# k and q loaded as twelve rows of one head per partition, and transposed by quarters of the array

## The chip, the cores and the metric

One core of one Trainium2 chip runs the whole program. The metric is the device time of one execution in microseconds (us), lower is better. The kernel before took 157.97 us, the median of three runs (157.73, 158.18 and 157.97). A change of about 0.3% (0.5 us) is what a measurement can tell from none.

## The reference, cut to what matters

Two stages. The first is a causal attention over 4 batches and 8 heads (768 rows of 64 values each), in which each query row sees only six of the 24 key chunks of 32 rows. A chunk is chosen by an upper bound of its scores, from the smallest and the largest key values in it. The second is a soft mixture of experts over the 3072 rows of 512 that come out of the attention.

```python
ub = sum(max(q * k_min, q * k_max), -1)           # 768 x 24 per head
top_chunks = argsort(where(causal, ub, -1e9))[..., -6:]
attn = softmax(where(sel & causal, q @ k.T / 8, -1e9))
x = (attn @ v) as 3072 x 512
logits = x @ phi                                   # 3072 x 32 slots
slot_out = relu((softmax0(logits).T @ x) @ w1) @ w2     # 8 experts, 4 slots each
out = softmax1(logits) @ slot_out
```

The inputs are float32: q, k and v have 6.3 MB each, the weights 33.5 MB.

## The kernel before, in words

The attention works on 16 pairs of heads, in a pipeline. The order of all work is written out by hand: ORDER and PLAIN are lists of step names for each turn i of the pipeline, and every engine runs its instructions in that order. One turn works on several pairs at once: scores S0 to S5, exponentials E0 to E5 and diagonal masks A0 to A5 for pair i, the bounds and the choice of chunks (UB, SL, SH, UN, NT, NC) for pair i+1, the transposes of k and q with what follows them (KT, KE, KN, KX, BD and QT, QE, QP) for pair i+2, the loads of k and q (LK, LQ) for pair i+4 and of v (LV) for pair i+2, and the product with v (P0 to P5), its normalising (NO) and its transposes (XT, XE) for the pairs before.

**Loads.** `load` (L158) is one DMA, issued by GpSimd (POOL), for k or q of one pair. It converts float32 to bfloat16 on the way. Partition p gets rows 6p to 6p+5 of the first head and then the same rows of the second head: two pieces of 1536 bytes in HBM, of 768 bytes in SBUF, for each of 128 partitions. `load_first` (L166) brings pair 0 as float32 through SyncE (SP), and `cast_first` (L172) converts it on VectorE and ScalarE, half a tile at a time. Of k_in and q_in there are three buffers each. v comes in pieces of 256 bytes (L180), the expert weights in rows of 8 KB in HBM (L156); the last two weight tiles come in halves of columns, as eight smaller DMAs (L154), at a time when tiles of the attention have been given up. All of these go through POOL.

**Transposes.** `transposes` (L234) turns such a tile so that the 64 values of a row lie on partitions: head 0 on partitions 0 to 63, head 1 on 64 to 127. For each of six row indices g and each head h it issues one weight load (128 rows, 64 columns of the tile) and one matmul with the identity as moving operand (128 columns), into half h of the PSUM tile tr_ps. That makes 12 matmuls per tile, 24 per pair. `evac_T` (L246) is one ScalarE (ACT) instruction, which copies tr_ps to kT or qT and puts the rows back into order on the way: it walks over p outside and over the six g inside.

**What uses kT and qT.** The scores (L342) and the masks added to them (L352) run on 64 rows of the array for each head, into one of two PSUM tiles sc_ps; ACT takes the exponential of them (L365); POOL cuts the diagonal (L370). VectorE (DVE) takes chunk minima and maxima of kT (L259, L264) and splits qT by sign (L279, L282); the bounds follow on the tensor engine (L291, L297), then the choice of the chunks on DVE (L303, L307, L316).

**The end.** After the last pair come the slot inputs, the first expert layer (L770), the second (L810) in two column halves, and the output rows (L840, evacuated on L847 and L849, sent by SP on L853).

Of the kernel before, what the change touches and what calls it, by code (L numbers as in the profile page):

```python
# [11 lines left out]
BF16 = mybir.dt.bfloat16  # L12
# [8 lines left out]
NQT = 6  # L21
P = 128
S = 768
D = 64
# [15 lines left out]
for _g, _pieces in enumerate(GROUPS):  # L40
# [4 lines left out]

PLAIN = """S0 KT S1 E0 A0 E1 LQ NO UB S2 S3 P0 KE LK SL P1 P2 P3 P4 E2 E3 A2 A1 W XT SH QT UN S4 S5 QE LV KN E4
E5 A5 A3 XE KX NT P5 NC BD QP A4 LG LC"""
# [4 lines left out]
LV A4 QP A5 BD""",  # L52
    1: """LV KT S0 LQ S1 LK UB E0 S2 E1 NO S3 P0 P1 A0 P2 SL KE SH E2 QT P3 A1 XT UN XE S4 W S5 KN E3 QE E4 E5
A5 P4 A2 KX A3 NT LG BD A4 NC P5 LC QP""",
    13: """S0 KT LV E0 S1 UB E1 A1 KE NO S2 S3 E2 E3 P0 P1 SL UN QT SH P2 QE P3 A3 A2 KN KX XT S4 S5 CL XE QP
E4 A0 W BD E5 P4 NT A5 LG P5 NC A4 LC MX""",
    14: """S0 E0 S1 UB S2 NO MT S3 RM P0 E1 E2 P1 E3 MB SL A1 A2 MS S4 MD A0 SH E4 UN P2 RS S5 XT P3 P4 A3 NT
NC E5 XE RE CU A4 A5 P5""",
    15: """NO S0 S1 C0 E0 S2 E1 P0 S3 E2 E3 V0 A1 XT P1 P2 A3 S4 A0 S5 P3 E4 A4 A2 E5 ME A5 P4 P5 XE""",
    16: """ZN0 ZPA ZP3 ZCT ZP4 D0 ZLH ZX0 ZN1 ZP5 Ze0 ZN2 D1 ZX1 ZL1 ZX2 D2 Ze1 ZL3 ZE2 ZL4 ZPM Zk ZPT ZMB D3  # L60
# [7 lines left out]
def kernel(  # L68
# [10 lines left out]
    nc = tc.nc  # L79
# [8 lines left out]
    EARLY = 12  # L88
    OLD = B - 1
    NO = OLD * NQT  # L90
    LAST = NPAIR - 1

    ctx.enter_context(tc.manual_schedule())
# [6 lines left out]
    p_tp = ps_ctx.enter_context(tc.tile_pool(name="p_tp", bufs=2, space=PSUM))  # L100
    st = {}
# [3 lines left out]
    ident = static.tile([P, P], BF16, name="ident")  # L105

    phi_sb = static.tile([P, NDG, NS], BF16, name="phi_sb")
    cT_all = static.tile([P, B * NQT, P], BF16, name="cT_all")
    c_pad = static.tile([P, NO, 4, CH], BF16, name="c_pad")
    lg_all = static.tile([P, OLD, NQT, NS], F32, name="lg_all")  # L110
# [28 lines left out]
    inp = l_ctx.enter_context(tc.tile_pool(name="inp", bufs=3, side="right"))  # L139
# [18 lines left out]
    def load(i, nm):  # L158

        b, j = divmod(i, NPB)  # L160
        t = inp.tile([P, 2, NQT * D], BF16, name=nm + "_in", tag=nm + "_in")
        src = {"k": k, "q": q}[nm][b, 2 * j:2 * j + 2]
        nc.gpsimd.dma_start(out=t, in_=src.rearrange("h (p g) d -> p h (g d)", p=P))  # L163
        st[nm, i] = t

    def load_first(nm):  # L166
        n = NQT * P // 2
        t = cT_all.rearrange("p t c -> p (t c)").bitcast(F32)[:, (nm == "q") * 2 * n:][:, :2 * n]
        st[nm + "f"] = t = t.rearrange("p (h x) -> p h x", h=2)
        nc.sync.dma_start(out=t, in_={"k": k, "q": q}[nm][0, :2].rearrange("h (p g) d -> p h (g d)", p=P))  # L170

    def cast_first(nm):  # L172
        t = inp.tile([P, 2, NQT * D], BF16, name=nm + "_in", tag=nm + "_in")
        nc.vector.tensor_copy(t[:, 0], st[nm + "f"][:, 0])  # L174
        (nc.scalar.copy if nm == "k" else nc.vector.tensor_copy)(t[:, 1], st[nm + "f"][:, 1])
        st[nm, 0] = t

    def load_v(i):
# [5 lines left out]


    load_first("k")
    load_first("q")
    for t in (ns_t[1], ns_t[0], caus, qgrp, headsel, squad):
        nc.vector.memset(t, 0.0)
# [8 lines left out]
    for n in "I K1 Q1 K2 Q2 W G M".split():  # L198
        if n[0] == "I":
            make_identity(nc, ident)  # L200
        elif n[0] == "W":
            load_w(0)
        elif n[0] == "V":
            load_v(int(n[1]))
        elif n == "G":
            nc.gpsimd.affine_select(
                out=qgrp, in_=qgrp, compare_op=ALU.not_equal, fill=1.0, base=0,
                pattern=[[-1, 4], [0, CH]], channel_multiplier=1,
            )
            nc.gpsimd.affine_select(  # L210
                out=caus[:4], in_=caus[:4], compare_op=ALU.is_ge, fill=NEG, base=0,
                pattern=[[0, 4], [-1, 4]], channel_multiplier=1,
            )
        elif n == "M":
            nc.gpsimd.affine_select(
                out=squad, in_=squad, compare_op=ALU.not_equal, fill=-NEG, base=0,
                pattern=[[-CH, 2], [-64, 2], [-1, NCHUNK]], channel_multiplier=1,
            )
            nc.gpsimd.affine_select(
                out=squad, in_=squad, compare_op=ALU.not_equal, fill=1.0, base=-NCHUNK,  # L220
                pattern=[[-CH, 2], [-64, 2], [0, NCHUNK]], channel_multiplier=1,
            )
        else:
            load(int(n[1]), n[0].lower())
# [8 lines left out]

    def transposes(i, nm):  # L234

        ps = p_tp.tile([P, NQT, P], BF16, name="tr_ps", tag="tp")
        src = st.pop((nm, i))
        for g in range(NQT):
            for h in range(2):
                nc.tensor.matmul(  # L240
                    ps[h * 64:(h + 1) * 64, g, :], lhsT=src[:, h, g * D:(g + 1) * D], rhs=ident,
                    is_transpose=True,
                )
        st[nm + "ps", i] = ps

    def evac_T(i, nm):  # L246

        t = tp3.tile([P, S], BF16, name=nm + "T", tag=nm + "T")
        nc.scalar.activation(  # L249
            t.rearrange("d (p g) -> d p g", g=NQT),  # L250
            st.pop((nm + "ps", i)).rearrange("d g p -> d p g"),
            func=ACT.Copy, scale=-1.0 if nm == "q" else 1.0,
        )
        st[nm + "T", i] = t
# [130 lines left out]
    def pv(i, ts):  # L385
        if i == LAST and ts[0] == 0:
            st["at", i] = p_tp.tile([P, 2, 3 * (D + 1)], F32, name="at_ps", tag="tp")
        elif i == LAST and ts[0] == 3:
            st["at_a"] = st["at", i]
            st["at", i] = last_home()[:, 0, :].rearrange("p (h c) -> p h c", h=2)  # L390
        elif ts[0] == 0:
            st["at", i] = p_at.tile([P, 2, 512], F32, name="at_ps", tag="at")
        at, tb = st["at", i], 3 if i == LAST and ts[0] > 2 else 0
        for t in ts:
            for h in range(2):
                o = at[:, h, (t - tb) * (D + 1):(t - tb + 1) * (D + 1)]
                for kg in range(t + 1):
                    g, c = BLOCK[(kg, t)]
                    nc.tensor.matmul(  # L399
                        o, lhsT=st["e", i, g][:, h, c:c + P], rhs=v_t[i % NV][:, h, kg, :],  # L400
                        start=(kg == 0), stop=(kg == t),
                    )
# [172 lines left out]
    def of(d, f, *a):  # L575
# [3 lines left out]
        "UB": of(1, ubound), "SL": of(1, search), "SH": of(1, shift), "UN": of(1, unselect),  # L579
        "NT": of(1, ns_transposes), "NC": of(1, evac_ns),  # L580
        "KT": of(2, transposes, "k"), "KE": of(2, evac_T, "k"), "KN": of(2, kmin), "KX": of(2, kmax), "BD": of(2, heads),
        "QT": of(2, transposes, "q"), "QE": of(2, evac_T, "q"), "QP": of(2, qsplit),
        "LK": of(4, load, "k"), "LQ": of(4, load, "q"), "LV": of(2, load_v), "Lv": of(1, load_v), "W": weights,
        "NO": of(-2, normalise), "XT": of(-2, x_transposes), "XE": of(-2, evac_x),
        "LG": lambda i: moe(moe_logits, i - 2), "LC": lambda i: moe(moe_copy, i - 2),
        "PHI": phi_load, "kc": lambda i: cast_first("k"), "qc": lambda i: cast_first("q"), "MASK": spread_mask, "CL": close_loads, "CU": close_bounds,
    }
    for g in range(len(GROUPS)):
# [130 lines left out]
    def slots_z():  # L719
# [9 lines left out]
    STEP.update({n: (lambda i, f=f, a=a: f(*a)) for n, f, *a in (  # L729
        ("ZCT", close_T), ("ZCE", close_e), ("ZCI", close_i), ("ZN0", normalise, LAST - 1),  # L730
        ("ZPA", pv, LAST, [0, 1, 2]), ("ZP3", pv, LAST, [3]), ("ZP4", pv, LAST, [4]), ("ZP5", pv, LAST, [5]),
        ("ZX0", x_transposes, LAST - 1), ("ZE0", evac_x, LAST - 1, 0, NQT, nc.vector.tensor_copy),
        ("Ze0", evac_x, LAST - 1, 0, NQT, nc.scalar.copy),
# [173 lines left out]
```

## Time and profile before

One profiled execution; its own time was 157.73 us, with a span of 155.8 us between its first and its last instruction.

| what | value |
|---|---|
| time of the profiled execution | 157.73 us |
| its span | 155.8 us |
| granted TensorE clock, mean | 0.964 |
| bytes read from HBM | 52.49 MB |
| bytes written to HBM | 6.29 MB |
| matmuls of L240 (the transposes) | 384, 229 ns each |
| ACT copies of L249 | 32, 815 ns (q) and 805 ns (k) each |
| loads of k and q by POOL | 30, 192 KB each in SBUF |

How to read it: PE is the tensor engine's matmuls, PEld its weight loads. A line such as L240 is a line of the kernel before. In a list in order of time the first number is the start in us from the span's beginning, the second the duration; x12 stands for twelve instructions told in one row, from the first one's start to the last one's end. Matmuls are pipelined, so that the duration of one (219 ns) is far longer than the step from one to the next. GB/s of the DMA engines counts the bytes as they arrive: a load that converts reads twice as many.

### The profile page before, as it was taken

What the parts mean: (1) busy time and instruction counts of PE and PEld (TensorE: products, weight loads), DVE (VectorE), ACT (ScalarE), POOL (GpSimd) and SP (SyncE); (2) the same over time, 40 slices, a digit from 0 to 9 for tenths busy, and PEclk for the clock granted to TensorE, in tenths of its full rate; (3) what the DMA queues carried; (4) which work ended last, traced back from release to release, by engine and by line L of the source; (5) the groups of instructions that cost most, each with busy time, mean ns of one, the idle gap of its engine ahead of it and who ended that gap; (6) DMA issues with size and microseconds to landing.
All of it is one profiled execution on the core that took longest, in us unless ns stands there. A gap on an engine that the chain in (4) does not pass through costs nothing.

```text
span 155.8 us, 6234 instructions
## 1 busy us (share of the span) xinstructions
PE 135.7 (87%) x2591; PEld 95.5 (61%) x2591; DVE 117.0 (75%) x408; ACT 123.5 (79%) x165; POOL 98.3 (63%) x196
## 2 busy tenths in 40 slices
PE   6649899998999999999999999998999999877700
PEld 3335467766776777676767766685759856545400
DVE  5766979988889889898888989899946343439900
ACT  3669999999899999999989999998796303447900
POOL 7959895977789687796977885855627970000000
PEclk9956999999999999999999999999999999999995
DMA  4999999999999999999999999999999999998995
GB/s 161 176 207 199 168 220 183 193 216 186 213 194 206 201 184 212 196 208 200 182 208 200 207 202 200 207 203 192 200 215 211 214 198 194 159 325 306 392 404 219
DMA packets 46251, 33.32 MB, mean 214 GB/s; under 512 B 26512, under 2 KB 41872, under 8 KB 46224
## 3 DMA queue, kind: packets, MB, share of 16 engines
q0 software_dynamic: 41552, 25.86, 115.1%
q1 hardware_dynamic: 4672, 7.08, 12.4%
q8 instruction: 20, 0.33, 0.8%
q14 instruction: 7, 0.06, 0.1%
HBM read 52.49 MB, written 6.29 MB: 377 GB/s over the span
## 4 chain that ended last, share of the span: by engine, by line
POOL 26%; PE 20%; ACT 16%; DMA 14%; issue 10%; DVE 9%; POOLq 0%; ACTq 0%; DVEq 0%
ACT e_sb L365 10%; POOL e_sb L370 9%; DMA w_sb<-in_moe_w_dram 7%; DMA k_in<-in_k_dram 7%; POOL v_t L180 4%; PE at_ps L399 3%; PE sc_ps L342 3%; POOL q_in L163 3%; POOL w_sb L156 3%; POOL k_in L163 3%; ACT kT L249 2%; PE sc_ps L352 2%; PE tr_ps L240 2%; PE warm_ps L230 2%; POOL w_sb L154 2%
## 5 line engine op out<-in xcount | busy, mean ns | idle before, releaser
L365 ACT ACTIVATE e_sb<-sc_ps 128x768 bf16<-128x768 f32 (+1 forms) x96 | 83.0, 925 | 3.3 <-PE sc_ps L352 2.1
L370 POOL TENSOR_SCALAR_AFFINE_SELECT e_sb<-e_sb 128x256 bf16<-128x256 bf16 x96 | 37.1, 409 | 24.4 <-ACT e_sb L365 22.2
L342 PE MATMUL sc_ps<-qT,kT 64*128 64x384 bf16 (+3 forms) x288 | 39.9, 295 | 1.0 <-ACT e_sb L365 0.6
L352 PE MATMUL sc_ps<-nsT,smask 64*128 64x384 bf16 (+2 forms) x320 | 39.4, 278 | 0.0
L399 PE MATMUL at_ps<-v_t,e_sb 128*128 128x65 bf16 x672 | 27.7, 194 | 0.0
L399 PEld LDWEIGHTS <-e_sb 128*128 128x128 bf16 x672 | 23.9, 98 | 5.8 <-issue 5.3
L342 PEld LDWEIGHTS <-kT 64*128 64x128 bf16 x288 | 16.0, 94 | 10.0 <-issue 4.4
L352 PEld LDWEIGHTS <-smask 64*128 64x128 bf16 x320 | 17.4, 95 | 3.7 <-issue 0.4
L180 POOL DMA_DIRECT2D v_t<-in_v_dram x16 | 16.5, 1034 | 0.0
L412 DVE TENSOR_TENSOR x_sb<-at_ps,inv 128x768 bf16<-128x768 f32 (+1 forms) x17 | 15.5, 910 | 0.6
L259 DVE TENSOR_REDUCE mm<-kT 128x24 bf16<-128x768 bf16 x16 | 15.1, 943 | 0.1
L264 DVE TENSOR_REDUCE mm<-kT 128x24 bf16<-128x768 bf16 x16 | 15.1, 943 | 0.0
L249 ACT ACTIVATE qT<-tr_ps 128x768 bf16<-128x768 bf16 x16 | 13.0, 815 | 2.1 <-PE tr_ps L240 2.0
L307 DVE MAX8 mx_t<-ub_ps 128x8 f32<-128x16 f32 (+4 forms) x160 | 14.4, 163 | 0.0
L249 ACT ACTIVATE kT<-tr_ps 128x768 bf16<-128x768 bf16 x16 | 12.9, 805 | 0.7 <-PE tr_ps L240 0.7
L163 POOL DMA_DIRECT2D k_in<-in_k_dram x15 | 10.9, 726 | 0.8 <-issue 0.5
L163 POOL DMA_DIRECT2D q_in<-in_q_dram x15 | 10.8, 717 | 0.2 <-issue 0.2
L432 DVE COPY xT_sb<-xT_ps 128x768 bf16<-128x768 bf16 (+1 forms) x15 | 8.1, 543 | 2.8 <-PE xT_ps L421 1.6
L156 POOL DMA_DIRECT2D w_sb<-in_moe_w_dram x14 | 10.1, 718 | 0.0
L240 PE MATMUL tr_ps<-ident,k_in 128*64 128x128 bf16 x192 | 8.7, 229 | 1.5 <-DMA k_in<-in_k_dram 1.3
L240 PEld LDWEIGHTS <-k_in 128*64 128x64 bf16 x192 | 6.1, 113 | 5.9 <-DMA k_in<-in_k_dram 3.2
L240 PE MATMUL tr_ps<-ident,q_in 128*64 128x128 bf16 x192 | 9.0, 229 | 0.6 <-DVE q_in L174 0.4
(129 smaller groups left out, 215.3 us busy)
## 6 DMA issues: line engine op xcount, KB each, us to landing
w_sb<-in_moe_w_dram POOLq DMA_DIRECT2D x14, 1024.0 KB, 12.2
v_t<-in_v_dram POOLq DMA_DIRECT2D x16, 192.0 KB, 11.2
out_dram<-o_sb SPq DMA_DIRECT2D x12, 256.0 KB, 4.0
out_dram<-w_sb SPq DMA_DIRECT2D x6, 512.0 KB, 4.2
k_in<-in_k_dram POOLq DMA_DIRECT2D x15, 192.0 KB, 9.1
q_in<-in_q_dram POOLq DMA_DIRECT2D x15, 192.0 KB, 9.1
w_sb<-in_moe_w_dram POOLq DMA_DIRECT2D x8, 256.0 KB, 11.3
cT_all<-in_k_dram SPq DMA_DIRECT2D x1, 384.0 KB, 3.1
```

The source lines that it names most:

```text
L163: nc.gpsimd.dma_start(out=t, in_=src.rearrange("h (p g) d -> p h (g d)", p=P))
L180: nc.gpsimd.dma_start(out=v_t[i % NV][:, :, :, :D], in_=v[b, 2 * j:2 * j + 2].rearrange("h (g p) d -> p h g d", p=P),)
L240: nc.tensor.matmul(ps[h * 64:(h + 1) * 64, g, :], lhsT=src[:, h, g * D:(g + 1) * D], rhs=ident, is_transpose=True,)
L249: nc.scalar.activation(t.rearrange("d (p g) -> d p g", g=NQT), st.pop((nm + "ps", i)).rearrange("d g p -> d p g"), func=ACT.Copy, scale=-1 ...
L259: nc.vector.tensor_reduce(mm[:, 0, 0, :], kT, axis=AX.X, op=ALU.min, negate=True)
L264: nc.vector.tensor_reduce(st["mm", i][:, 1, 0, :], kT, axis=AX.X, op=ALU.max)
L342: nc.tensor.matmul(ps[:, h, c:c + w], lhsT=kT[r, kg * P:(kg + 1) * P], rhs=qT[r, qs], start=True, stop=False,)
L352: nc.tensor.matmul(ps[:, h, c + (f - t0) * P:c + (l - t0) * P], lhsT=smask[r, x, kg].rearrange("p a b -> p (a b)"), rhs=nsT[r, (f - x * NJ ...
L365: nc.scalar.activation(e[:, :, :w], st.pop(("scps", i, g))[:, :, :w], func=ACT.Exp, scale=-scale)
L370: nc.gpsimd.affine_select(out=e[:, :, :P], in_=e[:, :, :P], compare_op=ALU.is_ge, fill=0.0, base=0, pattern=[[0, 2], [1, P]], channel_mult ...
L399: nc.tensor.matmul(o, lhsT=st["e", i, g][:, h, c:c + P], rhs=v_t[i % NV][:, h, kg, :], start=(kg == 0), stop=(kg == t),)
L412: nc.vector.tensor_tensor(st["x", b][:, t0:t1, 2 * j:2 * j + 2, :].rearrange("p t h d -> p h t d"), at[:, :, :, :D], inv.broadcast_to([P, ...
```

## The change

Partition p now gets twelve rows of one head: partitions 0 to 63 hold head 0 (rows 12p to 12p+11), partitions 64 to 127 head 1. In HBM a partition's data are one piece of 3072 bytes, in SBUF one of 1536 bytes. The transposes then work on 64 rows and 64 columns of the array: for each of twelve row indices and each head one weight load (64 rows, 64 columns) and one matmul with a 64 x 64 corner of the identity as moving operand (64 columns). Head 0 uses the quarter of the array at rows 0 and columns 0, head 1 the one at rows 64 and columns 64. That makes 24 matmuls per tile, 48 per pair. PSUM holds the same bytes; the ACT copy walks over twelve g inside instead of six. No step of the written order changes. Against the kernel before, the tensor engine has 768 instructions more (384 weight loads and 384 matmuls); DVE, ACT, POOL and SP have the same instructions in the same order with the same waits.

```diff
+    NG = 2 * NQT
 def load(i, nm):
-        t = inp.tile([P, 2, NQT * D], BF16, name=nm + "_in", tag=nm + "_in")
+        t = inp.tile([P, NG * D], BF16, name=nm + "_in", tag=nm + "_in")
-        nc.gpsimd.dma_start(out=t, in_=src.rearrange("h (p g) d -> p h (g d)", p=P))
+        nc.gpsimd.dma_start(out=t, in_=src.rearrange("h (p g) d -> (h p) (g d)", g=NG))
 def load_first(nm):
-        st[nm + "f"] = t = t.rearrange("p (h x) -> p h x", h=2)
-        nc.sync.dma_start(out=t, in_={"k": k, "q": q}[nm][0, :2].rearrange("h (p g) d -> p h (g d)", p=P))
+        st[nm + "f"] = t
+        nc.sync.dma_start(out=t, in_={"k": k, "q": q}[nm][0, :2].rearrange("h (p g) d -> (h p) (g d)", g=NG))
 def transposes(i, nm):
-        ps = p_tp.tile([P, NQT, P], BF16, name="tr_ps", tag="tp")
+        ps = p_tp.tile([P, NG, 64], BF16, name="tr_ps", tag="tp")
-        for g in range(NQT):
+        for g in range(NG):
             for h in range(2):
+                r = slice(h * 64, (h + 1) * 64)
                 nc.tensor.matmul(
-                    ps[h * 64:(h + 1) * 64, g, :], lhsT=src[:, h, g * D:(g + 1) * D], rhs=ident,
-                    is_transpose=True,
+                    ps[r, g, :], lhsT=src[r, g * D:(g + 1) * D], rhs=ident[r, r], is_transpose=True,
                 )
 def evac_T(i, nm):
-            t.rearrange("d (p g) -> d p g", g=NQT),
+            t.rearrange("d (p g) -> d p g", g=NG),
```

`cast_first` converts the same halves of the tile, written as columns of the flat tile.

More of the change, by code (lines that the diff above doesn't have):

```diff
@@ L168, in load_first @@
         t = cT_all.rearrange("p t c -> p (t c)").bitcast(F32)[:, (nm == "q") * 2 * n:][:, :2 * n]
-        st[nm + "f"] = t = t.rearrange("p (h x) -> p h x", h=2)
-        nc.sync.dma_start(out=t, in_={"k": k, "q": q}[nm][0, :2].rearrange("h (p g) d -> p h (g d)", p=P))
+        st[nm + "f"] = t
+        nc.sync.dma_start(out=t, in_={"k": k, "q": q}[nm][0, :2].rearrange("h (p g) d -> (h p) (g d)", g=NG))
     def cast_first(nm):
-        t = inp.tile([P, 2, NQT * D], BF16, name=nm + "_in", tag=nm + "_in")
-        nc.vector.tensor_copy(t[:, 0], st[nm + "f"][:, 0])
-        (nc.scalar.copy if nm == "k" else nc.vector.tensor_copy)(t[:, 1], st[nm + "f"][:, 1])
+        t = inp.tile([P, NG * D], BF16, name=nm + "_in", tag=nm + "_in")
+        n = NG * D // 2
+        nc.vector.tensor_copy(t[:, :n], st[nm + "f"][:, :n])
+        (nc.scalar.copy if nm == "k" else nc.vector.tensor_copy)(t[:, n:], st[nm + "f"][:, n:])
         st[nm, 0] = t
```

## The prediction, made before the changed kernel had run

> **What bounds the kernel now.** I read the page first, then the busy time by stage, then ACT in order of time over one pair, then the end of the chain. The page:
>
> ```profile
> PE 135.7 (87%) x2591; PEld 95.5 (61%) x2591; DVE 117.0 (75%) x408; ACT 123.5 (79%) x165; POOL 98.3 (63%) x196
> DMA  4999999999999999999999999999999999998995
> DMA packets 46251, 33.32 MB, mean 214 GB/s; under 512 B 26512, under 2 KB 41872, under 8 KB 46224
> ```
>
> No engine is full over the span, but the 16 DMA engines are nine tenths busy or more in nearly every slice. The stage of the pairs is read by windows (the last two numbers are DMA share and GB/s); the first row here is three whole pairs:
>
> ```profile
> core 0: us, PE busy (x) PEld busy (x) DVE busy (x) ACT busy (x) POOL busy (x), PEclk, DMA share, GB/s
> 61.00:80.40 19.40, 19.11 (x402) 13.94 (x398) 17.26 (x58) 18.79 (x24) 15.62 (x33) 1.00 1.41 199
> 118.00:124.00 6.00, 5.76 (x152) 5.30 (x148) 3.38 (x9) 1.95 (x4) 5.35 (x8) 1.00 1.07 214
> 128.00:134.00 6.00, 5.70 (x119) 3.60 (x110) 1.30 (x6) 1.82 (x5) 0.48 (x1) 1.00 1.45 196
> ```
>
> ACT is busy 18.79 of 19.40 us there. In order of time over one pair:
>
> ```profile
> 60.61 0.80 ACT L249 ACTIVATE kT<-tr_ps 128x768 bf16<-128x768 bf16 x1
> 61.30 1.95 ACT L365 ACTIVATE e_sb<-sc_ps 128x1024 bf16<-128x1024 f32 x2
> 63.26 0.81 ACT L249 ACTIVATE qT<-tr_ps 128x768 bf16<-128x768 bf16 x1
> 63.97 3.21 ACT L365 ACTIVATE e_sb<-sc_ps 128x768 bf16<-128x768 f32 x4
> 67.07 0.80 ACT L249 ACTIVATE kT<-tr_ps 128x768 bf16<-128x768 bf16 x1
> ```
>
> From kT to kT it has no gap: 67.07 - 60.61 = 6.46 us, the pitch of a pair. So ACT paces the pairs. The end is another matter:
>
> ```profile
> 127.74 10.80 DMA w_sb<-in_moe_w_dram
> 138.58 0.61 PE so_ps L810 x13
> POOL w_sb L154 <- DMA w_sb<-in_moe_w_dram: 0.9, 1, 0.9
> PE so_ps L810 <- DMA w_sb<-in_moe_w_dram: 0.7, 2, 0.4
> ```
>
> The last weight load is issued at 127.74 and lands 10.8 us later, though it has only 256 KB: it stands in a queue. PE waits for such loads twice, 0.7 us in all, after having done everything else it could. The tail is therefore bound by how much the DMA engines had still to move.
>
> **The DMA part.** What one piece of a transfer costs can be worked out. In 118 to 124 us the queue holds weight tiles with pieces of 4096 bytes in SBUF, and 214 GB/s arrive; in 128 to 134 us it holds the halves with pieces of 512 bytes, and 196 arrive. Per 1000 bytes that is 4.67 and 5.10 ns, with 0.24 and 1.95 pieces: 0.43 ns for 1.71 pieces, 0.25 ns each, and 4.61 ns per 1000 bytes without them. Test on the three pairs: two weight tiles and nine loads of 192 KB are 3.87 MB, in 2 x 256 + 6 x 256 + 3 x 1536 = 6656 pieces (the v loads have 1536 each): 17.8 + 1.7 = 19.5 us, against 19.40 in the row. So the queue is full among the pairs too, and its cost is bytes plus pieces.
>
> The change takes 128 of 256 pieces from each load, 128 x 0.25 = 32 ns; 30 loads by POOL give 0.96 us of DMA time, and the two first loads by SP 0.06. The low end is 0 (the pieces may hide behind one another); the high end twice that, 1.9 us, since the 0.25 ns rests on two windows whose rates differ by a tenth.
>
> The Trainium skill, "DMA: Bandwidth & Descriptors", section "Why small descriptors are slow (HBM only)", gives a fixed overhead of about 3 cycles per packet beside 32 bytes a beat; by it a piece of 1536 bytes read takes 48 + 3 and one of 3072 bytes 96 + 3, an estimate of 3% of each load, so some 0.8 us for the sum. The trace agrees in order of size.
>
> How much of the 0.96 us comes through? Among the pairs nothing: ACT paces them, and a load that lands earlier only waits. Its profit is a shorter queue behind the last weights. Those are issued when the attention gives up its tiles, with over 10 us of queue ahead of them, so they would land earlier by nearly all of it. Behind them PE has two waits of 0.7 us in all and then output rows that wait for the same half; I take four fifths, **-0.8 us**, with 0 and -1.6 as the ends.
>
> **POOL's issue time.**
>
> ```profile
> L163 POOL DMA_DIRECT2D k_in<-in_k_dram x15 | 10.9, 726 | 0.8 <-issue 0.5
> L180 POOL DMA_DIRECT2D v_t<-in_v_dram x16 | 16.5, 1034 | 0.0
> L370 POOL TENSOR_SCALAR_AFFINE_SELECT e_sb<-e_sb 128x256 bf16<-128x256 bf16 x96 | 37.1, 409 | 24.4 <-ACT e_sb L365 22.2
> ```
>
> From 256 to 1536 pieces the issue grows by 308 ns, 0.24 ns a piece, so 128 fewer give 31 ns per load, 0.06 us per pair. POOL waits 22.2 us for ACT in all, 1.4 us per pair, so this is worth nothing.
>
> **The PE part.** It removes 12 weight loads and 12 matmuls of 128 columns per tile and adds 24 and 24 of 64 columns; the same twice per pair. The group before, cut after two, four and twelve matmuls, and its weight loads cut after two and four:
>
> ```profile
> 62.69 0.25 PE L240 MATMUL tr_ps<-ident,q_in 128*64 128x128 bf16 x2
> 62.69 0.30 PE L240 MATMUL tr_ps<-ident,q_in 128*64 128x128 bf16 x4
> 62.69 0.53 PE L240 MATMUL tr_ps<-ident,q_in 128*64 128x128 bf16 x12
> 62.69 0.11 PEld L240 LDWEIGHTS <-q_in 128*64 128x64 bf16 x2
> 62.69 0.14 PEld L240 LDWEIGHTS <-q_in 128*64 128x64 bf16 x4
> ```
>
> The two heads run side by side in two column halves: a pair of matmuls adds (0.53 - 0.25) / 5 = 56 ns, about what 128 columns take. The second pair of weight loads ends 30 ns after the first. So six pairs take 6 x 56 = 336 ns of the array. What is the step of a pair of 64 columns in two quarters? No row shows it. From below it is half of 56, 28 ns. The nearest rows with one matmul at a time are these:
>
> ```profile
> 66.24 0.18 PE L291 MATMUL ub_ps<-bd,qm 128*128 128x48 bf16 x1
> 66.27 0.18 PE L291 MATMUL ub_ps<-bd,qp 128*128 128x48 bf16 x1
> 61.31 1.12 PE L399 MATMUL at_ps<-v_t,e_sb 128*128 128x65 bf16 x30
> L399 PE MATMUL at_ps<-v_t,e_sb 128*128 128x65 bf16 x672 | 27.7, 194 | 0.0
> ```
>
> 48 columns step by about 25 ns, 65 columns by (1.12 - 0.194) / 29 = 32 ns, each with a weight load of its own. If the quarters run side by side as the halves do, the step of a pair is 28 to 32 ns; I take 32, the row with nearly the same columns and a weight load each: 12 x 32 = 384 ns, +48 per tile, +0.10 us per pair. If they do not, each of 24 takes 25 to 32 ns: 600 to 768, +264 to +432 per tile. I take the first: rows (the scores' two heads) and columns (these transposes) each run side by side before.
>
> Is there room for +0.10 us? PE's row is as dense as ACT's, so I look for gaps:
>
> ```profile
> 61.04 0.34 PE L352 MATMUL sc_ps<-nsT,smask 64*128 64x384 bf16 x2
> 63.71 0.27 PE L342 MATMUL sc_ps<-qT,kT 64*128 64x256 bf16 x2
> 63.81 0.27 PE L352 MATMUL sc_ps<-nsT,smask 64*128 64x256 bf16 x2
> 64.15 0.34 PE L324 MATMUL ns_ps<-ident,ns_t 128*128 128x128 bf16 x3
> ...
> 60.41 0.38 PE L352 MATMUL sc_ps<-nsT,smask 64*128 64x128 bf16 x4
> 60.77 0.23 PE L342 MATMUL sc_ps<-qT,kT 64*128 64x128 bf16 x2
> ```
>
> Going over to another shape costs about 0.1 us after the last columns (61.04, 0.16 for 384 columns, next start 61.31 above). At 64.15 the columns of 63.81 had been done for 0.23 us, so 0.12 there is a wait, for the mask of another engine. The masks at 60.41 have 128 and 384 columns per head, 0.22 us, and the next scores, of the same shape, start 0.14 after that. Together about 0.25 us of room per pair. +0.10 fits: the sum has **0**, with 0 and +0.10 x 14 = +1.4 as ends. If that cover were gone, it would be the 1.4.
>
> The ACT copy starts later by the longer group less the shorter last matmul, 11 x 32 - 5 x 56 - 28, some 45 ns; ACT has exponentials ahead of it in its row, so nothing waits.
>
> **The ACT copy itself** has inner runs of 12 instead of 6, at steps of 64 instead of 128 elements in PSUM.
>
> ```profile
> L249 ACT ACTIVATE kT<-tr_ps 128x768 bf16<-128x768 bf16 x16 | 12.9, 805 | 0.7 <-PE tr_ps L240 0.7
> L529 ACT COPY cT_all<-cT_ps 128x768 bf16<-128x768 bf16 x1 | 0.8, 790 | 0.0
> ```
>
> A copy of the same size with no steps takes 790 ns, 15 less. As ACT paces the pairs it would count in full: 28 copies x 15 = 0.4 us either way. I take 0, with -0.4 and +0.4.
>
> **The start.** ACT's first cast waits 1.8 us for the first k, so there the SP load counts: 32 ns. The casts keep their size. -0.05.
>
> **Sum**, on the profiled execution's own time of 157.73 (span 155.8 and 1.9 around it): -0.8 - 0.05 = 156.9. The median of the runs is 0.24 above it, so the prediction for the median is **157.2 us**.
>
> **Rivals.** *A, the quarters take turns (slower).* The price is +264 ns per tile at 25 ns a matmul, +0.53 us per pair; beyond the 0.25 of room that is +0.28, over 14 pairs +3.9 us. It decides from a step of about 38 ns per pair of matmuls, (336 + 125) / 12, where the room is used up; at 32 ns a matmul it is +8.6. The queued weights would land while the attention is still late, so a part hides; at two thirds, 157.97 + 2.6 = 160.6, and up to 163.7. For it: the change doubles the instructions, and no row shows two weight loads and two matmuls within 30 ns. Against it: the two halves' weight loads step by 30 ns for 64 columns already.
>
> The Trainium skill, "TensorE: Matmul & The Clock Gate", Part 1 ("Wait — 56ns, not 53.3ns?"), says that the start-to-start of matmuls does not fall below about 25 ns however few columns they have. The rows with 48 columns agree; taken for each matmul it would give rival A, taken for each quarter the forecast. The transposes before show two starts within one 56 ns step, which speaks for the second reading as far as columns go.
>
> *B, nothing moves.* The pieces cost no time because byte movement hides them, or the time won at 138.58 is lost again in the outputs, which keep the DMA engines at nine tenths after it: 157.97, within 0.5. For it: the output stage. Against it: the test on three pairs.
>
> **How the numbers follow.** Forecast 0.53, rival A 0.28, rival B 0.19. About 0.3% (0.5 us) is what a measurement can tell from no change. So: faster 0.53, same 0.19, slower 0.28. The low end is the forecast with twice the DMA gain, 157.97 - 1.6 - 0.4 = 156.0; the high end takes in most of rival A, 161.0. The forecast's own range is 156.0 to 157.5.
>
> **What will show it.** In the changed profile: packets down by about 3840 from 46251; L240's group of 24 spanning about 0.55 us, against 0.75 or more under rival A; ACT's kT to kT at 6.46 us, against 6.7 or more under A; the last w_sb landing near 137.7; the two PE waits of 0.7 us on it smaller. A pitch above 6.5 us with a short group would mean that ACT's copy got dearer; fewer packets without an earlier landing would make the piece cost wrong.

## The result, and the profile after

The changed kernel took 165.17 us (median of 6 runs, 163.6 to 165.97) against 157.85 us before (6 runs, 157.71 to 159.0): a ratio of 1.0433, 95% interval 1.0371 to 1.0495. The prediction was 157.2, with a range up to 161.0: wrong, and on the other side. The profiled execution took 165.02 us, with a span of 163.1. Of the experiments below, the profiles of e3, e10 and e12 fell into executions with a disturbed clock and e10's ratio rests on its two undisturbed runs, so that lengths given for these three are rougher than the others.

The page of the kernel after. A step that stood on a line before stands one to three lines further down now: the transposes L240 are L243, the copy L249 is L251, the scores L342 are L344, the product with v L399 is L401, the loads L163 are L164.

```profile
span 163.1 us, 7002 instructions
PE 137.2 (84%) x2975; PEld 98.9 (61%) x2975; DVE 117.1 (72%) x408; ACT 123.7 (76%) x165; POOL 93.5 (57%) x196
DMA  5999999999999999999999999999999999679994
DMA packets 42158, 33.37 MB, mean 205 GB/s; under 512 B 26512, under 2 KB 37520, under 8 KB 42128
PE 65%; ACT 15%; issue 7%; DVE 4%; DMA 4%; POOL 0%; DVEq 0%; ACTq 0%; POOLq 0%
L251 ACT ACTIVATE qT<-tr_ps 128x768 bf16<-128x768 bf16 x16 | 13.0, 813 | 7.7 <-PE tr_ps L243 7.5
L251 ACT ACTIVATE kT<-tr_ps 128x768 bf16<-128x768 bf16 x16 | 12.9, 806 | 0.5 <-PE tr_ps L243 0.5
L243 PE MATMUL tr_ps<-ident,q_in 64*64 64x64 bf16 x384 | 9.9, 197 | 3.3 <-issue 1.7 <-DVE xT_sb L434 1.2 <-DVE q_in L176 0.4
L164 POOL DMA_DIRECT2D k_in<-in_k_dram x15 | 8.3, 556 | 0.5 <-ACT kT L251 0.2
```

PE was busy 135.7 us before and is busy 137.2 now, 1.5 us more; ACT is where it was. Yet the chain that ended last runs 65% through PE, and ACT waits 7.5 us for the transposes of q. So PE did not get much more to do: it stood still. The stage of the pairs by windows, before and then after (columns as in the windows of the prediction: us, then busy time and count of PE, PEld, DVE, ACT and POOL, the clock, the DMA share and GB/s):

```profile
26.00:108.00 82.00, 80.38 (x1637) 57.85 (x1636) 73.85 (x258) 79.69 (x99) 63.55 (x131) 1.00 1.40 200
```

```profile
26.00:115.00 89.00, 81.21 (x1895) 59.49 (x1890) 73.19 (x257) 78.41 (x98) 59.90 (x130) 1.00 1.34 193
```

As much work of ACT and DVE, or a little less, takes 89 us instead of 82, and PE is busy 0.83 us longer in it. Nearly all of the 7.3 us of span is lost here.

What the prediction had asked to see. The groups of 24 transposes, in PE's order of time, and ACT from kT to kT in the same pairs:

```profile
62.54 0.56 PE L243 MATMUL tr_ps<-ident,k_in 64*64 64x64 bf16 x24
66.46 0.57 PE L243 MATMUL tr_ps<-ident,q_in 64*64 64x64 bf16 x24
```

```profile
64.37 0.81 ACT L251 ACTIVATE kT<-tr_ps 128x768 bf16<-128x768 bf16 x1
65.06 1.95 ACT L367 ACTIVATE e_sb<-sc_ps 128x1024 bf16<-128x1024 f32 x2
67.07 0.81 ACT L251 ACTIVATE qT<-tr_ps 128x768 bf16<-128x768 bf16 x1
67.77 3.22 ACT L367 ACTIVATE e_sb<-sc_ps 128x768 bf16<-128x768 f32 x4
70.89 0.81 ACT L251 ACTIVATE kT<-tr_ps 128x768 bf16<-128x768 bf16 x1
```

The group spans 0.56 us where 0.55 was forecast, and 70.89 - 64.37 = 6.52 us where 6.46 was: in a pair that nothing disturbs, the change costs what the prediction said. It is other pairs that are late. The waits of the kernel after (line that waited, what for: us in total, times, longest), and below them the same groups before:

```profile
PEld L243 <- issue: 7.6, 18, 1.4
ACT qT L251 <- PE tr_ps L243: 7.5, 9, 1.7
PEld L401 <- issue: 7.0, 22, 1.0
PEld L344 <- issue: 5.0, 18, 0.8
```

```profile
PEld L399 <- issue: 5.3, 18, 0.3
PEld L342 <- issue: 4.4, 20, 0.5
PEld L240 <- issue: 2.4, 10, 0.3
```

"issue" means that the engine waited for nothing that the profile shows. The totals are not the sign, since PE has many short ones; the longest single waits are: 0.3 to 0.5 us before, 0.8 to 1.4 after, on three different kinds of work. They even stand in the middle of a group, where no other engine can be waited for:

```profile
86.93 0.37 PE L243 MATMUL tr_ps<-ident,q_in 64*64 64x64 bf16 x11
88.59 0.38 PE L243 MATMUL tr_ps<-ident,q_in 64*64 64x64 bf16 x13 [1.29 <-issue]
```

Eleven transposes, 1.29 us of nothing, then the other thirteen. Where do these stops stand? I numbered all of PE's records (weight loads, matmuls and 27 instructions of its sequencer) in the order of their starts and listed, between 20 and 128 us, the long steps from one start to the next. One remainder of the number by 256 stands out; its steps over 0.2 us are:

```
after: number of the record | us from its start to the next start
961   1.34     1729  0.61     3009  0.39     4033  0.79
1217  0.44     1985  0.67     3521  1.48     4289  0.96
1473  0.85     2241  0.61     3777  0.27     4545  1.14
                                              sum 9.55
```

Every one of these numbers leaves 193 when it is divided by 256; the steps over 0.2 us at any other remainder sum to 0.52 us at most. At its own such places the kernel before has one step over 0.2 us (0.21). And something comes in pieces of 256 instructions: the page's list of DMA queues has

```profile
q8 instruction: 23, 0.38, 0.9%
```

23 transfers, 0.38 MB, that is 16,384 bytes each, or 256 instructions of 64 bytes; and PE's records are 5977, which makes 23 blocks of 256 (5209 before, and 20 transfers). So I take it that q8 brings PE's own program, through the same DMA engines as the data. Each such transfer takes 0.95 us; and in the kernel after PE goes on 1.2 to 1.7 us behind the end of one (28.95 to 30.35, 34.98 to 36.35, 41.0 to 42.23 for the first three).

The Trainium skill, "Runtime: NRT & Kernel Launch", section "Instruction fetch mechanics", tells of the same thing: the instructions come in blocks of 16 KiB, 256 of them, by a DMA queue of the sequencer's own. It calls the crossing of a block "mostly hidden". The trace agrees with the block and its size; that it is hidden held for the kernel before (0.21 us) and not for this one (9.55).

### The profile page after: what moved, and what is told of

It reads as the page before. It is cut to its first block, busy times and chain, and to the rows that moved or that the text cites. A ratio compares the mean times of both kernels' runs of the same rounds, so it can differ in the third digit from the quotient of the medians.

```text
span 163.1 us, 7002 instructions
## 1 busy us (share of the span) xinstructions
PE 137.2 (84%) x2975; PEld 98.9 (61%) x2975; DVE 117.1 (72%) x408; ACT 123.7 (76%) x165; POOL 93.5 (57%) x196
## 2 busy tenths in 40 slices
DMA packets 42158, 33.37 MB, mean 205 GB/s; under 512 B 26512, under 2 KB 37520, under 8 KB 42128
## 4 chain that ended last, share of the span: by engine, by line
PE 65%; ACT 15%; issue 7%; DVE 4%; DMA 4%; POOL 0%; DVEq 0%; ACTq 0%; POOLq 0%
PE sc_ps L344 13%; PE at_ps L401 12%; PE tr_ps L243 9%; ACT e_sb L367 9%; PE sc_ps L354 9%; PE ub_ps L293 4%; DMA k_in<-in_k_dram 4%; PE xT_ps L423 3%; PE so_ps L812 3%; PE h_ps L772 2%; ACT qT L251 2%; PE o_ps L842 2%; ACT w_sb L851 2%; PE h_ps L511 1%; PE ns_ps L326 1%
## 5 line engine op out<-in xcount | busy, mean ns | idle before, releaser
L372 POOL TENSOR_SCALAR_AFFINE_SELECT e_sb<-e_sb 128x256 bf16<-128x256 bf16 x96 | 36.5, 402 | 35.7 <-ACT e_sb L367 34.6
L344 PE MATMUL sc_ps<-qT,kT 64*128 64x384 bf16 (+3 forms) x288 | 40.4, 295 | 2.0 <-issue 0.6
L401 PE MATMUL at_ps<-v_t,e_sb 128*128 128x65 bf16 x672 | 28.2, 194 | 1.3 <-issue 1.2
L401 PEld LDWEIGHTS <-e_sb 128*128 128x128 bf16 x672 | 24.1, 98 | 7.1 <-issue 7.0
L344 PEld LDWEIGHTS <-kT 64*128 64x128 bf16 x288 | 16.1, 94 | 9.9 <-issue 5.0
L354 PEld LDWEIGHTS <-smask 64*128 64x128 bf16 x320 | 16.6, 95 | 4.8 <-issue 1.6
L251 ACT ACTIVATE qT<-tr_ps 128x768 bf16<-128x768 bf16 x16 | 13.0, 813 | 7.7 <-PE tr_ps L243 7.5
L251 ACT ACTIVATE kT<-tr_ps 128x768 bf16<-128x768 bf16 x16 | 12.9, 806 | 0.5 <-PE tr_ps L243 0.5
L243 PE MATMUL tr_ps<-ident,q_in 64*64 64x64 bf16 x384 | 9.9, 197 | 3.3 <-issue 1.7
L243 PE MATMUL tr_ps<-ident,k_in 64*64 64x64 bf16 x384 | 9.8, 200 | 1.9 <-DMA k_in<-in_k_dram 1.5
L243 PEld LDWEIGHTS <-k_in 64*64 64x64 bf16 x384 | 7.8, 114 | 5.9 <-issue 3.8
L243 PEld LDWEIGHTS <-q_in 64*64 64x64 bf16 x384 | 7.8, 111 | 5.6 <-issue 3.8
L334 DVE COPY nsT<-ns_ps 128x384 bf16<-128x384 bf16 x16 | 5.7, 356 | 7.0 <-PE ns_ps L326 7.0
```

Source lines behind the costliest of these rows:

```text
L243: nc.tensor.matmul(ps[r, g, :], lhsT=src[r, g * D:(g + 1) * D], rhs=ident[r, r], is_transpose=True,)
L251: nc.scalar.activation(t.rearrange("d (p g) -> d p g", g=NG), st.pop((nm + "ps", i)).rearrange("d g p -> d p g"), func=ACT.Copy, scale=-1. ...
L344: nc.tensor.matmul(ps[:, h, c:c + w], lhsT=kT[r, kg * P:(kg + 1) * P], rhs=qT[r, qs], start=True, stop=False,)
L354: nc.tensor.matmul(ps[:, h, c + (f - t0) * P:c + (l - t0) * P], lhsT=smask[r, x, kg].rearrange("p a b -> p (a b)"), rhs=nsT[r, (f - x * NJ ...
L372: nc.gpsimd.affine_select(out=e[:, :, :P], in_=e[:, :, :P], compare_op=ALU.is_ge, fill=0.0, base=0, pattern=[[0, 2], [1, P]], channel_mult ...
L401: nc.tensor.matmul(o, lhsT=st["e", i, g][:, h, c:c + P], rhs=v_t[i % NV][:, h, kg, :], start=(kg == 0), stop=(kg == t),)
```

## The experiments

The theories, as the expectations name them:

- **T1, instruction supply.** The next block is called for when PE enters a new one, and takes some 6 us to come while the DMA queues are full. PE has 267 instructions per pair before (402 + 398 in three pairs, in the windows of the prediction) and 315 after. At 6.46 us per pair, 256 of them last 6.2 us before and 5.25 after. (The expectations say 261 and 309, reckoned from the steps between the blocks, and 5932 records where the trace has 5977.)
- **T2, the quarters cost array time** that does not show in the group (filling, draining, changing the shape).
- **T3, the new loads** collide with something.
- **T4, each added instruction costs the same**, in PE's dispatch, wherever it stands.

### e1 and e2: each half of the change alone

e1 has the new loads with the twelve old transposes, e2 the old loads with the quarters. In both the tiles' rows do not fit the transposes, so the attention works on other numbers.

```diff
 e1, from the kernel after
-        for g in range(NG):
+        for g in range(NQT):
...
-                    ps[r, g, :], lhsT=src[r, g * D:(g + 1) * D], rhs=ident[r, r], is_transpose=True,
+                    ps[h * 64:(h + 1) * 64, g, :], lhsT=src[:, (h * NQT + g) * D:(h * NQT + g + 1) * D], rhs=ident,
+                    is_transpose=True,
... (tr_ps and the copy by ACT in six again)
 e2, from the kernel before
-        for g in range(NQT):
+        for g in range(NG):
+                r = slice(h * 64, (h + 1) * 64)
...
-                    ps[h * 64:(h + 1) * 64, g, :], lhsT=src[:, h, g * D:(g + 1) * D], rhs=ident,
-                    is_transpose=True,
+                    ps[r, g, :], lhsT=src[r, g * D:(g + 1) * D], rhs=ident[r, r], is_transpose=True,
... (tr_ps and the copy by ACT in twelve)
```

> The new loads (one piece per partition) with the twelve 128-row transposes of the kernel before; so the rows in kT and qT stand in another order and partly under the other head, and the values that come out are others. PE has the instructions of the kernel before. Theory T1 (PE runs out of instructions: its program arrives in blocks of 256 instructions, and a block can't follow the last in less than about 6 us): no PE steps of 0.3 us or more at a fixed distance of 256 instructions, and no loss, 157.0 to 158.0. Rival T2 (64-row, 64-column transposes themselves cost array or drain time): the same, 157.0 to 158.0. Rival T3 (the new loads collide with other transfers, so k and q come late): about 165. The piece cost of the prediction by itself: 157.0, 0.8 below the kernel before; if pieces cost nothing, 157.85.

> The loads of the kernel before, two pieces per partition, with the 24 transposes by quarters; the order of the rows is again another, and the values too. T1: 5932 PE rows as in the changed kernel, so 163.5 to 166, with steps of 0.4 to 1.5 us at instructions 256 apart. T2: the same time, but with the loss spread over the groups of transposes (a group longer than 0.56 us or gaps round it), not at a distance of 256. T3: 157.9.

Measured: e1 156.96 us (156.52 to 157.28), ratio 0.9933 [0.9907, 0.996], 1.06 us under before; e2 166.69 us (165.29 to 167.76), ratio 1.0548 [1.0496, 1.06], 8.65 us over it. Of e1, the page and ACT in order of time:

```profile
DMA packets 42155, 33.32 MB, mean 215 GB/s; under 512 B 26512, under 2 KB 37520, under 8 KB 42128
L164 POOL DMA_DIRECT2D q_in<-in_q_dram x15 | 8.4, 560 | 0.6 <-PE sc_ps L354 0.5
```

```profile
61.20 0.81 ACT L251 ACTIVATE kT<-tr_ps 128x768 bf16<-128x768 bf16 x1
67.67 0.81 ACT L251 ACTIVATE kT<-tr_ps 128x768 bf16<-128x768 bf16 x1
```

The loads are a gain of the size forecast, the pitch stays at 6.47 us, and T3 falls. All of the loss, and more, belongs to the quarters: in e2 the long steps at 193 of 256 sum to 11.3 us (14 over 0.2 us).

### e3, e6 and e7: more instructions with the old transposes

48, 24 and 12 weight loads per pair are given twice, without their matmul; e3 does it in the scores and x_transposes too, e7 for q alone.

```diff
 e6, from the kernel before
             for h in range(2):
+                nc.tensor.ldweights(src[:, h, g * D:(g + 1) * D], is_transpose=True, tile_position=(0, h * 64))
                 nc.tensor.matmul(
```

> The kernel before with 48 weight loads more per pair, each a repeat of the one that follows it (24 in the transposes, 18 in the scores, 6 in the transposes of x): 5932 PE rows, as many as in the changed kernel, no quarters, the loads as before. T1: 163.5 to 166, with the same long steps 256 instructions apart. [...]

> The same with the 24 repeats in the transposes alone, about 285 PE instructions per pair instead of 261. T1: 256 instructions are used up in 256 / 285 x 6.46 = 5.8 us, about the time in which blocks followed one another in the changed kernel, so the loss has hardly begun: 158 to 160.5. A cost per instruction, linear in their number (T4: dispatch): half of the changed kernel's 7.3 us, so 161.5.

> The kernel before with 12 weight loads more per pair, repeats in the transposes of q alone: about 273 PE instructions per pair. T1: 256 instructions take 6.05 us at the pitch of 6.46, as long as a block's turn: 157.8 to 158.5. Linear cost per instruction (T4): a quarter of 7.3 us, 159.7.

Measured: e3 1.0582 [1.0536, 1.0627], e6 1.039 [1.0348, 1.0432], e7 1.0207 [1.0172, 1.0241], medians of 167.57, 163.91 and 160.97 us: dearer than their expectations made it under T1 or T4, and mostly not at the boundaries, whose steps over 0.2 us sum to 1.4 us in e6 and 0.5 in e7. The loss is elsewhere. Of e6, ACT and PE in order of time:

```profile
66.00 0.81 ACT L250 ACTIVATE qT<-tr_ps 128x768 bf16<-128x768 bf16 x1 [0.46 <-PE sc_ps L353]
```

```profile
65.01 0.55 PE L241 MATMUL tr_ps<-ident,q_in 128*64 128x128 bf16 x12
```

The group takes 0.55 us, as before, but ACT's copy of q waits for PE beyond it. Its waits in e6, and those of the kernel before:

```profile
ACT qT L250 <- PE sc_ps L353: 5.0, 10, 0.8
ACT qT L250 <- PE tr_ps L241: 2.0, 2, 1.6
```

```profile
ACT qT L249 <- PE tr_ps L240: 2.0, 2, 1.4
```

A weight load given on its own is tied in differently: in e6 as built, every added load and 371 of the 384 transposes raise PE's semaphore, where 19 transposes did before. So these three changed the signalling as well as the number, and tell nothing of T1 against T4. Whether it is the signalling that costs the time was not tried.

### e4 and e5: the same instructions, fewer weights in the queue

Weight tiles 1 to 11 are not loaded, and the experts that need them use tile 0, so the expert layers compute with other weights. e4 is the kernel after with this edit, e5 the kernel before. PE's instructions stay the same in number, kind and order.

```diff
 def load_w(i, ys=range(2)):
+        if 0 < i < EARLY:
+            return
...
-                    rhs=w_sb[e][:, dg * F + f * 512:dg * F + (f + 1) * 512],
+                    rhs=w_sb[e if e >= EARLY else 0][:, dg * F + f * 512:dg * F + (f + 1) * 512],
... (the second expert layer likewise)
```

> The changed kernel without the loads of the weight tiles 1 to 11; the experts that need them use tile 0, so the values are others. 11.5 of the 33.3 MB that the DMA engines move are gone while the pairs run. T1: a block of instructions waits less behind other transfers, the long steps 256 apart vanish or shrink below 0.3 us, and the time is within 1 us of the same edit on the kernel before (e5). T2 or a cost per instruction (T4): the instructions and the array's work are the same as in the changed kernel, so 6 to 8 us above e5.

> The same edit on the kernel before, as the measure for e4: ACT paces the pairs as before and the last loads find an empty queue, so 153 to 157. T1, T2 and T4 alike.

Measured, 10 runs each: e4 157.06 us (156.1 to 158.41), ratio 0.9948 [0.9924, 0.9972] to the kernel before; e5 156.53 (155.61 to 157.5), 0.9922 [0.9897, 0.9946]. By the medians the change costs 0.5 us with the queues half empty; with full queues, 7.3. The stage of the pairs in e4, and its waits:

```profile
26.00:108.00 82.00, 81.11 (x1936) 60.08 (x1935) 74.28 (x260) 80.13 (x100) 53.95 (x122) 1.00 0.81 86
```

```profile
PEld L402 <- issue: 5.3, 18, 0.3
PEld L244 <- issue: 4.5, 15, 0.4
PEld L345 <- issue: 3.8, 17, 0.4
```

At a DMA share of 0.81 instead of 1.34, PE does the whole work of the changed kernel (1936 matmuls) in the 82 us of the kernel before, no wait on issue is longer than 0.4 us, and at the numbers that leave 193 no step is longer than 0.14 us. T2 and T4 fall: the instructions, the quarters and their order are the same, and the time is gone. From the trace, the parts of a block's way between 20 and 115 us (medians): PE enters a block, and the transfer of the next starts 3.08 us later in the kernel before, 3.66 after, 0.70 in e4, 0.24 in e5. Then follow 0.95 us of transfer and 1.2 to 1.7 us until PE runs on, if PE is already waiting.

### e8, e9 and e10: other doses of the change

Here the loads and the transposes fit each other again: the change in the odd pairs (e8), in every fourth pair (e9), or for k alone (e10), the rest as before; loads and copies choose by the same condition, which is i % 4 == 1 in e9 and nm == "k" in e10.

```diff
 e8, from the kernel before
+    def quartered(i):
+        return i % 2 == 1
 def transposes(i, nm):
+        if quartered(i):
+            ps = p_tp.tile([P, NG, 64], BF16, name="tr_ps", tag="tp")
+            for g in range(NG):
+                for h in range(2):
+                    r = slice(h * 64, (h + 1) * 64)
+                    nc.tensor.matmul(
+                        ps[r, g, :], lhsT=src[r, g * D:(g + 1) * D], rhs=ident[r, r], is_transpose=True,
+                    )
... (the loads and the copy by ACT under the same condition)
```

> New loads and quarters in the odd pairs alone; the even pairs as before. PE gets 48 instructions more in every second pair, 24 more per pair on average (285, against 261 before and 309 after). T1 (supply in blocks of 256, one block in about 5.8 to 6.0 us while the DMA queues are full): 285 per 6.46 us ask for a block every 5.80 us, just at the limit; 157.0 to 160.0, with stalls at 193 mod 256 of less than half of the 9.5 us of the changed kernel. T4 (each added instruction costs the same): half of what the quarters alone cost, +4.4, and half of what the loads gain, -0.45: 161.8, and no steps at the block boundaries.

> New loads and quarters in pairs 1, 5, 9 and 13 alone. 12 instructions more per pair on average (273). T1: a block is asked for every 6.06 us, later than it takes; 157.2 to 157.9, the time before or a little under it, with at most 2 us of steps at the boundaries. T4: a quarter of +8.8, less a quarter of 0.9: 159.8.

> New loads and quarters for k in every pair; q as before. 24 instructions more in each pair, evenly (285). T1: a block is asked for every 5.80 us in every pair, at the limit: 157.0 to 159.5, no worse than with the same number in odd pairs alone, where the pairs of 309 ask for one every 5.35. T4: 161.8.

Measured: e8 161.87 us, ratio 1.0251 [1.0224, 1.0277]; e9 159.07 us, 1.0091 [1.0066, 1.0116]; e10 162.69 us, 1.0205 [1.0158, 1.0251], which by the ratio is 160.8. T1 as I had put it, with one threshold for the average pair, is wrong: e9 should have cost nothing. T4's numbers (161.8, 159.8, 161.8) come nearer. But T4 had fallen with e4, and the place of the loss speaks against it again. All doses, worked out from the traces (used: us in which PE runs through 256 instructions, median; steps: long steps at 193 of 256 over 0.2 us, number and sum; over before: (ratio - 1) x median of before):

```
                  used   steps        over before
before            6.43   1   0.2 us
e1 loads alone    6.35   1   0.2      -1.06 us
e9 every fourth   6.05   3   1.7      +1.43
e10 k alone       5.78   6   3.7      +3.23
e8 odd pairs      5.80   6   4.6      +3.96
after             5.45  12   9.6      +6.83
e2 quarters alone 5.42  14  11.3      +8.65
```

The steps less before's 0.2, less the loads' 1.06 in proportion, give e9 1.2, e10 3.0 and e8 3.8 us, against 1.43, 3.23 and 3.96, each within the interval of its run: the long steps account for the time at these doses. (In the two largest they sum to more than is lost, 8.3 for 6.83 and 11.1 for 8.65; that PE would have waited anyway in part of that time is likely and not shown.) So the supply is short or not for each block by itself, and not on average. The smallest dose shows it best; e9's PE in order of time:

```profile
62.85 0.53 PE L250 MATMUL tr_ps<-ident,q_in 64*64 64x64 bf16 x21
63.85 0.24 PE L250 MATMUL tr_ps<-ident,q_in 64*64 64x64 bf16 x3 [0.46 <-issue]
```

This block was used up in 4.99 us, from 58.20 to 63.19, since pair and boundary fell so that 45 of the pair's 48 quarter transposes and few scores and masks (26 of them, 30 to 43 in the other blocks of e9 before 102 us) stood in one block; the next was there 5.65 us after 58.20. The blocks of e9 that PE used in 6.03 us or more cost nothing, but for one of 0.13 us. Of the eight used in less, three cost more, those used in 4.99, 5.78 and 5.48 us: there the next transfer started 3.19 to 4.11 us after PE had entered the block. The other five, used in 4.97 to 5.97 us, cost nothing: there it started after 2.68 to 3.10 us. So the turn itself (from the entry of one block to the entry of the next) is no constant: where PE stood waiting over 0.2 us, a block came 5.65 to 6.81 us after the one before in the kernel after, 4.9 to 6.5 in the three doses. Averages hide both spreads; their tails are what the small dose pays. One step of each dose (0.34 us in e9, 0.95 in e8, 0.81 in e10) stands behind the attention, in a block without a transpose: there the added instructions had only shifted the boundaries.

### e11 and e12: what does the block wait for?

```diff
 e11, from the kernel after
-            src = moe_w1[i].rearrange("(a p x) f -> p a (x f)", p=P, x=2)
-            dst = w_sb[i].rearrange("p (a f) -> p a f", a=NDG // 2)
+            src = moe_w1[i].rearrange("(a p) f -> p a f", p=P)
+            dst = w_sb[i].rearrange("p (a f) -> p a f", a=NDG)
... (the weights of the second layer likewise)
 e12, from the kernel after
-            nc.gpsimd.dma_start(out=dst, in_=src)
+            for a in range(2):
+                nc.gpsimd.dma_start(out=dst[:, a], in_=src[:, a])
```

> The changed kernel, with the 14 whole weight tiles in pieces of 2048 bytes of SBUF instead of 4096, 512 per tile instead of 256, still one transfer per tile. The rows of the weights stand in another order for it, so the expert layers multiply other rows; nothing else changes. What does the instruction block wait for, 2.5 to 4.4 us, before its transfer starts? Q1, a fixed number of pieces ahead of it on its DMA engine: the wait goes with the size of a piece and falls to about 2 us, the long steps at the block boundaries from 9 us to under 3, and with 14 x 256 x 0.25 ns = 0.9 us more for pieces 158.5 to 161. Q2, the share of one whole transfer on its engine (64 KB of a weight tile, 4.7 us at the 13.5 GB/s of a sixteenth of 216): the transfer is as large as before, so 165 to 166.5. Q3, all that is queued, however it is cut: 165 to 166.5.

> The changed kernel, with each of the 14 whole weight tiles as two transfers of 512 KB one after the other, in the same pieces of 4096 bytes. Q2 (share of one transfer): the wait of an instruction block halves to about 2 us, the long steps fall under 3 us, and the time to 157.5 to 160. Q1 (number of pieces) and Q3 (all that is queued): the steps stay, 165 to 166.5. POOL issues 14 transfers more at some 0.7 us each, which its idle time covers.

Measured: e11 166.85 us, ratio 1.0569 [1.0494, 1.0645]; e12 164.28 us, 1.039 [1.0347, 1.0433]. The wait before a block's transfer keeps its median, 3.62 and 3.77 us against 3.66, and the long steps sum to 11.1 and 10.4 us. Q1 and Q2 fall as far as the weight tiles go; the loads of q, k and v kept their pieces. Of the three, Q3, that the block waits behind what is queued however it is cut, is what is left. It is not shown by more than that and e4. (By its range of 165 to 166.5, e11 came out 0.4 us too slow and e12 0.7 too fast.)

The Trainium skill, "DMA: Bandwidth & Descriptors", section "Queues, rings and completion order", has each DMA engine take turns among its queues packet by packet, some 9 to 17 descriptors each. If a descriptor is one of these pieces, e11 should have shortened the wait; 3.62 against 3.66 us does not bear that out.

No version that computes the same beats the kernel before: the best of them, e9, is 0.9% slower.

## Why the prediction was wrong, step by step

- **The DMA part** (-0.8) was right: e1 gives -1.06 by its ratio, -0.91 by the medians, and the packets fell by 46251 - 42158 = 4093 (3840 by POOL's loads, 256 by the two first ones, less three more blocks of instructions). As forecast, the list of waits of e1 has no wait of PE for w_sb any more.
- **POOL's issue time** was mis-sized without harm: 726 to 556 ns for a load of k, 170 less instead of 31. The 0.24 ns per piece, taken between loads of different shape, is not what halving the pieces of one load saves (1.3 ns a piece).
- **The ACT copy** (0) was right: 806 and 813 ns, where it was 805 and 815.
- **The PE part** (0, with +1.4 as the end) is the step that failed. Its array price was right: a group of 24 in 0.56 us, 32 ns per pair of quarters forecast and 2 x (0.56 - 0.197) / 23 = 32 measured, and it fits into PE's room, as e4 and e5 show (0.5 us between their medians). What the step left out is that 48 more instructions per pair must also be brought to PE. The step counted them by the time that they occupy the array, and took the room from gaps in time. The room in supply was smaller: 256 instructions last 6.43 us before and 5.45 after, and a block's turn is around 6 us.
- **What could have been seen beforehand** is this line on the page of the kernel before:

```profile
q8 instruction: 20, 0.33, 0.8%
```

  One block in some 6.5 us among the pairs, on DMA engines that are nine tenths busy: a resource that the change asks more of, and no term of the sum named it. How long a block takes to come, the line does not say.
- **Rival A** had the sign and not the mechanism. It decides from a step of 38 ns per pair of matmuls; the step was 32, and the quarters do run side by side: a group of 0.56 us, not 0.75. The floor of about 25 ns from the Trainium skill's page "TensorE: Matmul & The Clock Gate", Part 1, is thus not one from each matmul to the next: in the trace two matmuls in two quarters start 3 to 4 ns apart. Within one quarter the step is 32 ns, which the floor allows and does not test. "A pitch above 6.5 us with a short group would mean that ACT's copy got dearer" was wrong too: the copy is the same, and against the same pairs before the pitch grows only where a block is late (by 1.54 us from kT at 84.8, with the step of 1.48 in it; by 0.06 at 64.4, with none over 0.2).
- **The last w_sb landing near 137.7** did not come about in the kernel after, since the attention ended some 8 us later (its last exponential at 125.66 us, 117.79 before). In e1, where it did not, PE's matmuls on that half wait for no weights.

## What to carry to other kernels

An instruction has a second price beside its time on the engine: its bytes have to come. Where the DMA queues are kept full and PE runs short matmuls, count PE's instructions per microsecond before adding any: here 256 in 6.4 us went unnoticed, three blocks of e9 used in 5.0 to 5.8 us cost 0.9%, and 256 in 5.4 us throughout cost 4%. A stop that stands at a fixed remainder of 256 in the engine's own numbering, on any kind of work and with no releaser, was the sign of it here.

## What the runs showed that was not expected

- A block of 256 instructions takes 4.9 to 6.8 us from the entry of one to the entry of the next when PE waits for it: 2.6 to 4.4 us until its transfer starts, 0.95 for the transfer, 1.2 to 1.7 until PE runs on. In the kernel after, at a DMA share of 1.34, it is 5.65 to 6.81; the shortest, 4.9 and 5.0 in e10 and e8, stand behind the attention at a share of 1.06. At a share of 0.81 (e4) the transfer starts after 0.7 us (median).
- Two quarters of the array, each with a weight load of 64 columns and a matmul of 64, step together by 32 ns, so 16 ns a matmul on average.
- A load of 192 KB in 128 pieces of 1536 bytes is issued by POOL in 556 ns, in 256 pieces of 768 bytes in 726.
- With weight loads given on their own nearly every transpose behind them raises the semaphore in the program as built (371 of 384 in e6 instead of 19), and 24 of them per pair cost 3.9% [3.48, 4.32] although the group of transposes keeps its 0.55 us.
